# Reordering the loads and casts of the output weights, and the start of the second pair, in a retention and gated-FFN kernel

## The chip, the cores and the metric

The kernel runs on one core of one Trainium2 chip. The metric is the device time of the program in microseconds (us), as the median of several executions. The span that a profile gives, from the first to the last instruction, is about 1.7 us shorter than the time of the same execution (344.3 for 345.99 us in the profile of the kernel before).

Beside each time stands the mean granted clock of TensorE over that execution, as a share of full speed. In this case it turned out to matter: two executions of one kernel on one chip differ by over 7 us, and those that differ have different clocks (346.25 us at 1.0 and 353.74 us at 0.971, both in c_before). I call an execution one at full clock where that mean is 0.999 or 1.0, and compare such executions with each other wherever I explain a difference of the schedule.

## The reference

The first half is retention: attention with a causal mask that decays with distance, without softmax. The second half is a feed-forward net with a sigmoid gate over all 8 × 576 = 4608 tokens.

```python
# q, k, v: (8 batches, 8 heads, 576, 64) float32
scores = scale * q @ k.transpose(0, 1, 3, 2)
gamma = 1.0 - 2.0 ** (-5.0 - np.arange(H))
Dmat = where(rel >= 0, gamma[:, None, None] ** rel, 0.0)   # rel = i - j
attn = (scores * Dmat) @ v
x = attn.transpose(0, 2, 1, 3).reshape(4608, 512)
gate = 1 / (1 + exp(-(x @ w_gate)))          # w_gate, w_val: (512, 1536)
out = (gate * (x @ w_val)) @ w_out           # w_out: (1536, 512)
```

The decay factors into gamma^i on q and gamma^-j on k. So a chunk of 128 tokens needs scaled q and k, a triangular mask, and a running state (the sum of k times v of the chunks before it).

## The kernel before

There are 40 attention steps, one per batch and chunk (the fifth chunk of a batch is only 64 tokens). I count steps and output rows from 0. "Chunk five" is the sixth chunk, that is, step 5. Steps 0 to 3 are done as two pairs at the start, with another layout. Every later step goes through the same supply chain: SyncE loads k, q and v; GpSimd (POOL) scales them to bf16; a transposing DMA turns k and q; then TensorE (PE) multiplies.

All early loads are issued in one fixed order on one queue, through a pool of 18 buffers:

```python
    load_pair(0)
    load_pair(1)
    for f in range(0, NFC, 2):
        load_w(f, 2)            # gate and value weights
    load(4)
    for f in range(6):
        load_wo(f)              # output-weight rows 0 to 5, 256 KB each
    load(5)                     # chunk five
    for f in range(6, NFC):
        load_wo(f)              # output-weight rows 6 to 11
```

The supply chain of a later step, with the turn by DMA:

```python
    def casts_to(s):
        while done["cast"] <= min(NS - 1, s):
            x = done["cast"]
            loads_to(x + (1 if x < 16 else 2))
            cast_k(x)           # POOL, 4 instructions
            cast_q(x)           # POOL
            cross(x)            # DMA transpose of k and q, tile T
            cast_v(x)           # POOL
            done["cast"] += 1
```

Steps 4 and 5 are turned on PE instead (`turn`). The hidden layer of the first 512 tokens runs in two halves of columns, `fill(n)` is n matmuls on zeros that keep PE busy, and the first output stage is this:

```python
    for s in (4, 5):
        cast_k(s); cast_q(s); cast_v(s)
        if s == 4:
            for f in range(6):
                cast_wo(f, on_pool)     # rows 0 to 5 on POOL
    ...
    for fc in range(NFC):
        if fc == 2:
            turn(4, [on_act])
        if fc == 7:
            turn(5, [on_act, on_dve])
        if fc in (4, 6, 8, 9, 10, 11):
            advance(at + 1)             # one phase of steps 4 and 5
        if fc > 5:
            cast_wo(fc, on_act if fc % 2 else on_dve)   # rows 6 to 11, just in time
        for nb in range(4):
            nc.tensor.matmul(opps[nb], lhsT=gvs[fc][:, nb * P:(nb + 1) * P], rhs=wo_sb[:, fc, :],
                             start=(fc == 0), stop=(fc == NFC - 1))
        if fc == 7:
            cast_dense(5, 0)
            cast_dense(5, 1)
```

A phase of kind `st` is a state update: four matmuls on PE, then two copies of the state by VectorE (DVE). So DVE's queue holds, in order, a copy that needs PE, then a cast that PE needs (in the trace of this kernel two copies at 52.70 and 53.15 us, then the cast of an output-weight row at 53.61).

## Time and profile before

| | before |
|---|---|
| time, median of 3 | 349.4 us (348.04 to 349.63) |
| the execution that was profiled | 345.99 us, span 344.3 us, clock 1.0 |
| PE busy | 328.6 us of the span (95%) |
| first output stage on PE | 41.9 to 61.2 us |

There is a tension in the first two rows that the prediction passed over, and it comes back later: the profiled execution is 2 us faster than the fastest of the three timed ones.

Two views carry more than the prediction shows. First lines of the page of the kernel before: the span, the clock that TensorE was granted (tenths of full speed, 40 slices), and the group of the first block's output products (busy time, mean ns of one, then the idle time of the engine just before them and what ended most of it).

```profile
span 344.3 us, 7601 instructions
...
PEclk9999999999999999999999999999999999999999
...
L680 PE MATMUL op<-wo_sb,gv 128*128 128x512 bf16 x48 | 11.9, 378 | 5.8 <-DVE wo_sb L198 2.8
```

The clock was full throughout this execution. PE stood idle for 5.8 us in front of the 48 products of the first output stage, and nowhere else in one group for as long. The list of waits of the first 62 us of the kernel before (total us, times, longest) says for what:

```profile
PE op L680 <- DVE wo_sb L198: 2.8, 2, 1.4
...
PE op L680 <- ACT wo_sb L198: 2.6, 2, 1.4
```

Four waits of 1.2 to 1.4 us, each for the cast of an output-weight row (`wo_sb`), two by DVE and two by ScalarE (ACT).

### The profile page before, as it was taken

What the parts mean: (1) busy time and instruction counts of PE and PEld (TensorE: products, weight loads), DVE (VectorE), ACT (ScalarE), POOL (GpSimd) and SP (SyncE); (2) the same over time, 40 slices, a digit from 0 to 9 for tenths busy, and PEclk for the clock granted to TensorE, in tenths of its full rate; (3) what the DMA queues carried; (4) which work ended last, traced back from release to release, by engine and by line L of the source; (5) the groups of instructions that cost most, each with busy time, mean ns of one, the idle gap of its engine ahead of it and who ended that gap; (6) DMA issues with size and microseconds to landing.
All of it is one profiled execution on the core that took longest, in us unless ns stands there. A gap on an engine that the chain in (4) does not pass through costs nothing.

```text
span 344.3 us, 7601 instructions
## 1 busy us (share of the span) xinstructions
PE 328.6 (95%) x2868; PEld 188.6 (55%) x2868; DVE 167.0 (49%) x350; ACT 171.1 (50%) x352; POOL 186.5 (54%) x333
## 2 busy tenths in 40 slices
PE   7899885998999999999999999999999999999996
PEld 3574342786956656656656655544555455544443
DVE  5758413564747626616527625550575255503320
ACT  6564333665755646436554655454554445324321
POOL 7533759968879885695258985591667500000000
PEclk9999999999999999999999999999999999999999
DMA  8999998999999999999929999992996430020002
GB/s 217 316 347 287 249 270 166 190 170 195 202 197 242 206 219 283 195 236 213 202 79 225 174 209 253 192 186 93 202 194 126 120 82 0 2 91 30 2 30 91
DMA packets 169716, 60.13 MB, mean 175 GB/s; under 512 B 151120, under 2 KB 163664, under 8 KB 169680
## 3 DMA queue, kind: packets, MB, share of 16 engines
q1 hardware_dynamic: 169536, 59.52, 82.6%
q8 instruction: 22, 0.36, 0.5%
q14 instruction: 14, 0.11, 0.2%
q10 hardware_dynamic: 144, 0.13, 0.1%
HBM read 37.75 MB, written 9.44 MB: 137 GB/s over the span
## 4 chain that ended last, share of the span: by engine, by line
PE 89%; ACT 3%; DVE 3%; POOL 2%; issue 1%; DMA 1%; POOLq 0%; ACTq 0%; DVEq 0%
PE h L476 53%; PE op L542 23%; PE op L680 3%; PE pv L400 2%; PE qk L379 2%; PE pv L398 2%; PE st L412 2%; DVE sbd L418 1%; POOL kp L216 1%; DMA k32p<-in_k_dram 1%; PE op L532 1%; PE pvp L362 1%; ACT vs L257 0%; DVE pt L381 0%; ACT sbd L341 0%
## 5 line engine op out<-in xcount | busy, mean ns | idle before, releaser
L476 PE MATMUL h<-xT,wv_sb 128*128 128x512 bf16 (+3 forms) x584 | 117.5, 324 | 0.7 <-ACT g L500 0.7
L476 PE MATMUL h<-xT,wg_sb 128*128 128x512 bf16 (+3 forms) x584 | 117.5, 324 | 0.2 <-DVE gv L504 0.2
L226 POOL TENSOR_TENSOR qk_nat<-k,ktab 64x256 bf16<-64x256 f32 x128 | 78.5, 613 | 54.3 <-PE st L412 27.7
L504 DVE TENSOR_TENSOR gv<-g,h 128x512 bf16<-128x512 bf16 (+1 forms) x106 | 66.3, 626 | 67.6 <-PE h L476 53.7
L500 ACT ACTIVATE g<-h 128x512 bf16<-128x512 f32 (+1 forms) x106 | 58.1, 549 | 75.6 <-PE h L476 68.6
L542 PE MATMUL op<-wo_sb,gv 128*128 128x512 bf16 x360 | 82.8, 379 | 0.0
L418 DVE CAST sbd<-st 64x256 bf16<-64x256 f32 x112 | 47.1, 420 | 50.3 <-PE st L412 47.8
L476 PEld LDWEIGHTS <-wg_sb 128*128 128x128 bf16 x584 | 51.3, 98 | 36.3 <-issue 0.4
L476 PEld LDWEIGHTS <-wv_sb 128*128 128x128 bf16 x584 | 51.1, 98 | 33.7 <-issue 1.0
L247 POOL CAST vbd<-v 64x256 bf16<-64x256 f32 x128 | 50.6, 395 | 14.2 <-PE pv L400 9.3
L542 PEld LDWEIGHTS <-gv 128*128 128x128 bf16 x360 | 33.3, 98 | 35.1
L257 ACT CAST vs<-v 64x256 bf16<-64x256 f32 x112 | 45.1, 403 | 1.7
L514 ACT COPY ob<-op 128x512 f32<-128x512 f32 x33 | 19.2, 585 | 43.4 <-PE op L542 40.8
L236 POOL TENSOR_TENSOR qk_nat<-q,qtab 128x512 bf16<-128x512 f32 (+1 forms) x36 | 37.5, 1043 | 2.8
L402 ACT CAST xT<-pv 128x512 bf16<-128x512 f32 (+1 forms) x36 | 19.3, 537 | 29.0 <-PE pv L400 29.0
L381 DVE TENSOR_TENSOR pt<-qk,tri 128x512 bf16<-128x512 f32 (+1 forms) x36 | 22.6, 629 | 19.9 <-PE qk L379 19.4
L412 PEld LDWEIGHTS <-qk_nat 128*128 128x128 bf16 x224 | 13.9, 98 | 11.4 <-POOL vbd L247 1.3
L400 PE MATMUL pv<-pt,vbd 128*128 128x64 bf16 x256 | 19.1, 193 | 0.6 <-DVE pt L381 0.6
L398 PE MATMUL pv<-T,sbd 128*128 128x64 bf16 x228 | 18.5, 193 | 0.0
L400 PEld LDWEIGHTS <-vbd 128*128 128x128 bf16 x256 | 16.4, 98 | 3.8
L398 PEld LDWEIGHTS <-sbd 128*128 128x128 bf16 x228 | 15.9, 98 | 3.4 <-issue 0.8
L680 PE MATMUL op<-wo_sb,gv 128*128 128x512 bf16 x48 | 11.9, 378 | 5.8 <-DVE wo_sb L198 2.8
(72 smaller groups left out, 176.4 us busy)
## 6 DMA issues: line engine op xcount, KB each, us to landing
out_dram<-ob SPq DMA_DIRECT2D x35, 256.0 KB, 2.4
k<-in_k_dram SPq DMA_DIRECT2D x28, 256.0 KB, 4.1
q<-in_q_dram SPq DMA_DIRECT2D x28, 256.0 KB, 4.7
v<-in_v_dram SPq DMA_DIRECT2D x28, 256.0 KB, 5.1
wg<-in_moe_w_gate_dram SPq DMA_DIRECT2D x12, 256.0 KB, 6.0
wv<-in_moe_w_val_dram SPq DMA_DIRECT2D x12, 256.0 KB, 6.3
wo<-in_moe_w_out_dram SPq DMA_DIRECT2D x12, 256.0 KB, 5.8
k32p<-in_k_dram SPq DMA_DIRECT2D x4, 256.0 KB, 4.4
```

Of the source, the lines that this page charges most:

```text
L226: nc.gpsimd.tensor_tensor(out=kn[half(hh), j, :, half(hh)], in0=k32[half(j), hh::2, :], in1=ktab[half(j), c, hh::2].unsqueeze(2).to_broadc ...
L236: nc.gpsimd.tensor_tensor(out=qs[0:n], in0=q32[0:n], in1=qtab[0:n, c, :].unsqueeze(2).to_broadcast([n, H, D]), op=ALU.mult)
L247: nc.gpsimd.tensor_copy(out=vb[half(hh), j, :, half(hh)], in_=v32[half(j), hh::2, :])
L257: nc.scalar.copy(out=natural["vs", s][half(hh), j], in_=loaded[s][2][half(j), hh::2, :])
L381: nc.vector.tensor_tensor(out=pt[:, :, 0:n].rearrange("p m (j t) -> p m j t", t=64), in0=qkp[:, :, 0:n].rearrange("p m (j t) -> p m j t", ...
L398: nc.tensor.matmul(pvp[:, m, half(j)], lhsT=before[:, m, :], rhs=qT[:, m, half(j)], start=True, stop=False)
L400: nc.tensor.matmul(pvp[:, m, half(j)], lhsT=vb[:, j, m, :], rhs=pt[:, m, half(j)], start=before is None, stop=True)
L418: nc.vector.tensor_copy(out=sb[half(hh), :, half(hh)], in_=st_tiles[b][half(hh)])
L476: nc.tensor.matmul(out, lhsT=w_sb[:, kc, fc * P:(fc + 1) * P], rhs=xT[:, kc, t0 + a:t0 + e], start=(kc == 0), stop=(kc == NKC - 1))
L500: nc.scalar.activation(out=g[:, 0:n], in_=h1[:, 0:n], func=AF.Sigmoid)
L504: nc.vector.tensor_tensor(out=gvs[some[0]][:, a:e], in0=g[:, 0:n], in1=h2[:, 0:n], op=ALU.mult)
L542: nc.tensor.matmul(opp, lhsT=gvs[fc][:, nb * P:(nb + 1) * P], rhs=wo_sb[:, fc, :], start=(fc == 0), stop=(fc == NFC - 1))
```

## The change

The intent: load chunk five ahead of all output weights; take the six casts away from POOL and let DVE and ACT make all twelve, alternating, in the order in which the rows land, and ahead of the copies that wait for PE; do the turns of chunks four and five earlier; and in the second pair, order turns and copies by when their data come, with fewer fill matmuls.

```diff
     load(4)
-    for f in range(6):
-        load_wo(f)
     load(5)
-    for f in range(6, NFC):
+    for f in range(NFC):
         load_wo(f)
@@ second pair @@
-    fill(2)
+    fill(1)
     pair_pv(0, 0, 1)
     pair_pv(0, 1, 0)
-    pair_out(0, 0, on_act)
     cast_pair("q", 1, 0, dve)
     pair_t("k", 1, 1, ffn_psum, "ffn", on_act)
+    pair_t("q", 1, 0, ffn_psum, "ffn", on_act)
     pair_pv(0, 1, 1)
     cast_pair("q", 1, 1, dve)
-    pair_out(0, 1, on_dve)
+    pair_out(0, 0, on_dve)
     pair_st(0, 1)
     tile_sv(1, on_act)
 ...
-    pair_t("q", 1, 0, ffn_psum, "ffn", on_act)
-    fill(3)
     pair_t("q", 1, 1, ffn_psum, "ffn", on_act)
+    pair_out(0, 1, on_act)
     pair_qk(1, 0, qk_psum, "qk")
     pair_qk(1, 1, ffn_psum, "ffn")
-    fill(4)
 ... (a fill(2) later, and one weight cast moved)
@@ hidden layer and first output stage @@
+        if f == 8:
+            for s in (4, 5):
+                cast_k(s); cast_q(s); cast_v(s)
+        if f == 10:
+            cast_wo(0, on_dve)
+            turn(4, [on_act])
 ...
-        if s == 4:
-            for f in range(6):
-                cast_wo(f, on_pool)
 ...
+    cast_wo(1, on_act)
+    cast_wo(2, on_dve)
+    advance(at + 1)
 ...
+    cast_wo(3, on_act)
     for fc in range(NFC):
+        if fc == 1:
+            advance(at + 1)
+            cast_wo(4, on_dve)
         if fc == 2:
-            turn(4, [on_act])
-        if fc == 7:
+            cast_dense(5, 0)
+            cast_dense(5, 1)
+            cast_wo(5, on_act)
+            cast_wo(6, on_dve)
+            cast_wo(7, on_act)
+            cast_wo(8, on_dve)
+        if fc == 4:
             turn(5, [on_act, on_dve])
-        if fc in (4, 6, 8, 9, 10, 11):
+            cast_wo(9, on_act)
+            cast_wo(10, on_dve)
+            cast_wo(11, on_act)
+        if fc in (5, 6, 7, 9):
             advance(at + 1)
-        if fc > 5:
-            cast_wo(fc, on_act if fc % 2 else on_dve)
 ... (the two cast_dense(5, ...) behind row 7 go)
```

More of the change, by code (lines that the diff above doesn't have):

```diff
@@ L625 @@
     pair_pv(1, 0, 0)
+    fill(2)
     pair_pv(1, 0, 1)
     cast_w("v", 0, 2, 0, on_act)
-    cast_w("v", 0, 2, 1, on_dve)
     pair_pv(1, 1, 0)
@@ L631 @@
     pair_pv(1, 1, 1)
+    cast_w("v", 0, 2, 1, on_dve)
     pair_out(1, 1, on_dve)
@@ L652 @@
         next_w(f + 2)
+        if f == 8:
+            for s in (4, 5):
+                cast_k(s)
+                cast_q(s)
+                cast_v(s)
+        if f == 10:
+            cast_wo(0, on_dve)
+            turn(4, [on_act])
         h_first((f + 1,), 0, 4 * P)
@@ L655 @@
             nc.vector.memset(zero.pop(0), 0.0)
-    for s in (4, 5):
-        cast_k(s)
-        cast_q(s)
-        cast_v(s)
-        if s == 4:
-            for f in range(6):
-                cast_wo(f, on_pool)
     done["cast"] = 6
@@ L681 @@
                              start=(fc == 0), stop=(fc == NFC - 1))
-        if fc == 7:
-            cast_dense(5, 0)
-            cast_dense(5, 1)
     for nb in range(4):
```

## The prediction

> **What bounds the kernel now.** I read the page first, then busy time by stretches of 10 us, the list of waits of the first 62 us, the chain that ended last, and the timelines of single engines, with the landing times of the single transfers that the trace keeps beside each issue.
>
> ```profile
> PE 328.6 (95%) x2868; PEld 188.6 (55%) x2868; DVE 167.0 (49%) x350; ACT 171.1 (50%) x352; POOL 186.5 (54%) x333
> ...
> PE   7899885998999999999999999999999999999996
> ```
>
> TensorE is the bound: 328.6 of 344.3 us. Only its idle time, or filler matmuls on its path, can be won, and the digit row (busy tenths of 8.6 us slices) puts the weak spots into the first quarter. By stretches of 10 us (columns: PE, PEld, DVE, ACT, POOL, clock, DMA share, GB/s):
>
> ```profile
> 40.00:50.00 10.00, 9.58 (x70) 5.05 (x69) 2.20 (x4) 2.12 (x5) 7.76 (x14) 1.00 1.06 273
> 50.00:60.00 10.00, 4.88 (x47) 2.57 (x45) 3.66 (x8) 4.45 (x9) 7.64 (x13) 1.00 0.84 162
> 60.00:70.00 10.00, 8.85 (x132) 7.20 (x132) 5.89 (x18) 5.92 (x15) 9.04 (x18) 1.00 1.01 193
> ```
>
> From 50 to 60 us PE does 4.88 us of work. The chain of waits names the cause:
>
> ```profile
> 50.95 0.53 ACT wo_sb L198
> 51.52 1.02 PE op L680 x4
> 52.70 0.42 DVE sbd L418
> 53.15 0.43 DVE sbd L418
> 53.61 0.44 DVE wo_sb L198
> 54.09 1.02 PE op L680 x4
> ```
>
> PE waits for the cast of an output-weight row; that cast stands in DVE's or ACT's order behind a copy that itself waits for PE. There are four such gaps, of 1.39, 1.42, 1.41 and 1.20 us: 5.4 us. The weights were long there: rows 6 to 11 landed at 45.5, 46.2, 46.8, 49.0, 49.7 and 50.4 us, but were cast at 47.1, 50.9, 53.1, 53.6, 57.3 and 59.6. It is an order problem, not a transfer problem.
>
> The second place is the start of the hidden layer:
>
> ```profile
> 16.04 1.04 PE L132 MATMUL idle<-blank 128*128 128x512 bf16 x4
> ...
> 18.71 0.43 DVE L193 CAST wv_sb<-wv 128x512 bf16<-128x512 f32 x1 [0.69 <-DMA wv<-in_moe_w_val_dram]
> ...
> 20.26 0.61 PE L476 MATMUL h<-xT,wg_sb 128*128 128x256 bf16 x4
> ```
>
> Filler matmuls stand before the second pair's last state update, and the first weights end landing at 18.69 us, 1.57 us before PE uses them.
>
> [...] a 256 KB tile of k, q or v (256-byte packets) lands every 1.0 to 1.2 us, an output-weight tile (2 KB packets) every 0.66 to 0.76. [...] SyncE issues the transpose of step 11 (count from 0) at 84.15 us, just after POOL's scaling of that step's q ends at 84.12. [...]
>
> **The change, part by part.**
>
> (a) *Second pair.* Fillers go from 2+3+4 to 1+2 in this stretch, six fewer, but most fill waits. The four before the state update (16.04 to 17.08) are on the path and go; the turn of the second q comes about 1 us earlier, so I place the state update near 15.6 instead of 17.0 and its pair's last products near 18.2. The first hidden group then waits for landed weights: DVE cast done near 19.1. So the hidden layer starts effectively at 18.7 instead of 20.26: 1.5 us. The single gap at 36.88 (0.69 us) may go or stay.
>
> (b) *Load order.* Chunk five (the sixth) moves ahead of all output weights. Its three tiles took 3.24 us to land (41.56 to 44.80). The fifth chunk's v lands at 37.63, so the sixth is there near 40.9 and output row 0 near 41.5 (before: 38.10), then one row per 0.67 us: row 5 near 45, row 11 near 49 to 50.5, since the bytes before it are the same. The first output product, at 41.88 before, needs row 0: 41.5 + 0.43 for the cast. What (a) won is therefore lost in a wait for row 0; the output stage starts at 42, as before.
>
> (c) *Casts.* Six POOL casts of 0.61 us (3.4 us together) leave POOL, six more go to DVE and ACT. POOL had 3.39 us of waiting for k at 51.65, so this frees nothing on the path. All casts now stand ahead of the copies that wait for PE. The stage then takes PE's own time: 48 matmuls in groups of four at 0.865 us (10.4), the turn of chunk five (0.65), and its scores, states and values (about 0.9), plus some 1 us of waiting for the fourth step's masked scores and the first rows: 13 us, so PE ends it at 55 to 56 instead of 61.32. Shift there: 5.3 to 6.3 us.
>
> (d) *What that shift meets.* Every later attention step needs a chain: load, POOL casts, transpose by DMA. It starts with the load of step 6, behind the last output row in both kernels; k landed at 51.52, and I expect 50.5 to 51.5. From there POOL works without a break to step 9:
>
> ```profile
> 51.65 2.85 POOL L226 TENSOR_TENSOR qk_nat<-k,ktab 64x256 bf16<-64x256 f32 x4 [3.39 <-DMA k<-in_k_dram]
> ...
> 63.06 2.63 POOL L226 TENSOR_TENSOR qk_nat<-k,ktab 64x256 bf16<-64x256 f32 x4
> ...
> 80.36 2.64 POOL L226 TENSOR_TENSOR qk_nat<-k,ktab 64x256 bf16<-64x256 f32 x4 [0.40 <-DMA k<-in_k_dram]
> ```
>
> Then it waits for k of step 10, landed at 74.36 behind the eighth step's transpose, and of step 11 (80.20). None of this depends on how fast PE is. So the chain gains at most what k of step 6 gains, about 0.5 us. The slack before PE's use, landing of the turned tile to first score matmul: step 7: 65.64 to 72.11, 6.5 us; step 8: 70.56 to 76.03, 5.5; step 9: 77.32 to 83.22, 5.9; step 10: 83.60 to 87.63, 4.0; step 11: 90.45 to 93.69, 3.2; step 12: 94.82 to 102.62, 7.8; later ones over 8.
>
> ```profile
> 84.15 2.74 SPq L263 DMA_TRANSPOSE T<-qk_nat  x1
> ...
> 93.69 0.40 PE L379 MATMUL qk<-T 128*128 128x64 bf16 x8
> ```
>
> The least slack decides: step 11 lets PE come 3.2 us earlier plus the chain's own 0.5. Of 5.3 to 6.3 us won, 1.6 to 2.6 come back as waits for turned tiles between 70 and 92 us. After that PE runs at its own rate to the end. The sum is −3.7 us: 349.4 − 3.7 = 345.7 us, 1.1% less.
>
> **The rivals.** *The chain follows and the whole shift stays:* then 343.1 to 344.1, and with the 0.69 us gap gone too somewhat less. For it: POOL loses 3.4 us of casts and the loads are issued from fewer freed buffers late. Against it: POOL was waiting for data just then, and the transfer share was 1.06 from 40 to 50 us, so no earlier landing is in sight. *The output weights become the bound:* if row 0 lands at 43 or a late row blocks DVE ahead of the state copies (row 10 at 49.7 in the old trace), the stage ends at 57; step 11 still decides, so this costs little unless it delays the load of step 6; with step 6 a microsecond late the result is 346.7. *Nothing gained:* moving the weights behind chunk five could starve the first products by all of its 3.24 us and the in-order queues of ACT and DVE, now full of casts waiting for landings, could hold up sigmoids; then 348 to 350. Against it: each row lands in 0.67 us, products need 0.865 us per row.
>
> **Range and chances.** Centre 345.7. The low end takes most of the shift and an earlier step 6 (343.4), the high end a later one and a stall of 1 us that I missed (347.8). Faster by over 2% needs under 342.4 us, 7.0 us, more than the whole of the shift at the output stage: 0.07. Slower by 2% needs a new wait of 10 us: 0.01.
>
> **What would show it.** In the profile after: the hidden layer starts 1 to 2 us earlier; PE waits for output row 0 near 40 to 42 us; no wait of PE for output-weight casts over 0.5 us once the stage runs; busy PE in 50 to 60 us over 8.5 us; POOL still starts step 6 at 50.5 to 51.7; new PE waits, ended by the transposes, of together 1.6 to 2.6 us before the scores of steps 8 to 11. I am wrong if k of step 6 lands over 1.5 us earlier or later, if turned tiles land earlier by the whole shift, or if PE has a gap of over 2 us before the first output product.

## The result, and the profile after

| | before | after |
|---|---|---|
| median | 349.12 us (348.04 to 349.63, 4 runs) | 339.69 us (338.85 to 340.25, 4 runs) |
| ratio of fast runs | | 0.9732 (0.97 to 0.9763) |
| profiled execution, span | 344.3 us, clock 1.0 | 338.5 us, clock 1.0 |
| PE begins the hidden layer | 20.26 us | 19.35 us |
| first output product | 41.88 us | 41.76 us |
| PE begins the next hidden layer | 61.16 us | 55.39 us |

A ratio is the mean time of one kernel's fast runs over that of the other's of the same rounds, so it is not quite the ratio of the medians. A run counts as slow, and is left out of the ratio, when it is over 1.5% above the fastest of its kernel.

The change is faster by 2.7%; I had given that 7 chances in 100. The time is 3.7 us below the low end of the range (343.4).

Page of the kernel after, the lines that answer to those of before:

```profile
span 338.5 us, 7556 instructions
...
PE   7899989889999999999999999999999999999996
...
PEclk9999999999999999999999999999999999999999
```

The slice with busy digit 5 (51.6 to 60.2 us) is gone. Busy time by stretches of 10 us of the kernel after, with the same columns as in the prediction:

```profile
40.00:50.00 10.00, 8.88 (x70) 4.67 (x69) 4.83 (x11) 6.98 (x13) 4.81 (x8) 1.00 1.03 336
50.00:60.00 10.00, 9.87 (x121) 7.16 (x121) 5.08 (x15) 4.20 (x10) 7.76 (x14) 1.00 1.01 193
60.00:70.00 10.00, 9.06 (x156) 7.29 (x155) 6.45 (x19) 7.30 (x18) 9.12 (x17) 1.00 0.91 174
```

From 50 to 60 us PE now works 9.87 us, where it worked 4.88. The list of waits of its first 62 us:

```profile
DVE wo_sb L196 <- DMA wo<-in_moe_w_out_dram: 5.2, 6, 1.4
...
ACT wo_sb L196 <- DMA wo<-in_moe_w_out_dram: 3.1, 3, 2.0
...
PE pv L398 <- DVE pt L379: 0.9, 1, 0.9
```

The casts now wait for the landing of their row, and no line has PE waiting for a cast of an output-weight row any more. Within the stage PE keeps one wait of 0.9 us, for the masked scores of step 4. Single instructions of the kernel after, in its timeline (start, duration, engine, line, operation, and in brackets the idle time before it and what ended that):

```profile
17.93 0.43 DVE L191 CAST wv_sb<-wv 128x512 bf16<-128x512 f32 x1 [0.52 <-DMA wv<-in_moe_w_val_dram]
...
19.35 0.61 PE L474 MATMUL h<-xT,wg_sb 128*128 128x256 bf16 x4
...
41.28 0.43 DVE L196 CAST wo_sb<-wo 128x512 bf16<-128x512 f32 x1 [1.09 <-DMA wo<-in_moe_w_out_dram]
...
41.76 1.25 PE L691 MATMUL op<-wo_sb,gv 128*128 128x512 bf16 x4
...
43.97 0.19 PE L398 MATMUL pv<-pt,vbd 128*128 128x64 bf16 x1 [0.92 <-DVE pt L379]
...
70.26 0.40 PE L377 MATMUL qk<-T 128*128 128x64 bf16 x8
...
87.91 0.40 PE L377 MATMUL qk<-T 128*128 128x64 bf16 x8
```

So far this is nearly the profile that I had predicted. One line is missing: PE was to wait for output row 0, and the list has no such wait. The scores of step 4 begin at 41.41 us, the first product stands at 41.76, and the cast of row 0 ends at 41.28 + 0.43 = 41.71, so row 0 can have cost PE about 0.2 us. The last two lines are the surprise: they are the first score matmuls of steps 8 and 11, at which I expected PE to stand still, and no wait is in front of either. The whole 5.77 us that PE won by the end of the stage (61.16 to 55.39) are still there at the end: 344.3 − 338.5 = 5.8. The trace's records of single transfers show why there was no wait:

| | before: landed, used, slack | after: landed, used, slack |
|---|---|---|
| turned tile of step 8 | 70.56, 76.03, 5.5 us | 70.02, 70.26, 0.2 us |
| turned tile of step 9 | 77.32, 83.22, 5.9 | 75.92, 77.44, 1.5 |
| turned tile of step 10 | 83.60, 87.63, 4.0 | 80.94, 81.86, 0.9 |
| turned tile of step 11 | 90.45, 93.69, 3.2 | 87.49, 87.91, 0.4 |
| k of step 10 (loaded) | 74.36 | 71.66 |

Step 8's tile comes 0.5 us earlier, as I had said of all of them. Those of steps 9, 10 and 11 come 1.4, 2.7 and 3.0 us earlier. PE just gets by, with 0.2 us to spare at step 8 and 0.4 at step 11.

The step at which the chain came forward most is the tenth. POOL's first scaling of its k, before and after, in the two timelines:

```profile
74.52 2.63 POOL L226 TENSOR_TENSOR qk_nat<-k,ktab 64x256 bf16<-64x256 f32 x4 [2.78 <-PE pv L400]
...
71.82 2.64 POOL L224 TENSOR_TENSOR qk_nat<-k,ktab 64x256 bf16<-64x256 f32 x4 [0.63 <-DMA k<-in_k_dram]
```

The view ends the first wait by PE, which would be another cause: POOL held up by PE itself. The trace's records speak against it. POOL's semaphore instruction that waits for this k ends at 74.43 us, 0.07 us behind its landing, and the scaling starts 0.10 us later, just as at 51.65 and 80.36 us, where the view names k. So both waits ended with the landing of k.

Two questions remained. Why did the chain of loads and turns come earlier, when POOL began it only 0.2 us earlier (51.46 for 51.65)? And why do the times differ by 349.12 − 339.69 = 9.4 us, but the profiles by 5.8 us?

### The profile page after: what moved, and what is told of

The parts are those of the page before. It is cut to its first block, busy times and chain, and to the rows that moved or that the text cites. A ratio compares the mean times of both kernels' runs of the same rounds, so it can differ in the third digit from the quotient of the medians.

```text
span 338.5 us, 7556 instructions
## 1 busy us (share of the span) xinstructions
PE 325.6 (96%) x2829; PEld 187.8 (55%) x2862; DVE 168.5 (50%) x353; ACT 172.5 (51%) x355; POOL 183.2 (54%) x327
## 4 chain that ended last, share of the span: by engine, by line
PE 83%; DMA 7%; issue 2%; ACT 2%; POOL 2%; DVE 1%; SPq 1%; POOLq 0%; ACTq 0%
PE h L474 49%; PE op L540 23%; DMA q<-in_q_dram 2%; PE pv L398 2%; PE pv L396 2%; DMA wo<-in_moe_w_out_dram 2%; PE qk L377 2%; PE st L410 2%; DMA k32p<-in_k_dram 2%; PE op L691 1%; POOL qk_nat L224 1%; DMA k<-in_k_dram 1%; SPq L91 1%; PE op L530 1%; ACT vs L255 1%
## 5 line engine op out<-in xcount | busy, mean ns | idle before, releaser
L540 PE MATMUL op<-wo_sb,gv 128*128 128x512 bf16 x345 | 81.6, 379 | 0.8
L512 ACT COPY ob<-op 128x512 f32<-128x512 f32 x33 | 19.2, 585 | 44.3 <-PE op L540 38.6
L410 PE MATMUL st<-vs,qk_nat 128*128 128x64 bf16 x224 | 15.6, 193 | 1.5 <-DVE sbd L416 0.8
```

Of the source, the lines that this page charges most:

```text
L410: nc.tensor.matmul(st_tiles[b][:, m, :], lhsT=natural["k", s][:, j, m, :], rhs=natural["vs", s][:, j, m, :], start=(c == 0 and j == 0 and ...
L540: nc.tensor.matmul(opp, lhsT=gvs[fc][:, nb * P:(nb + 1) * P], rhs=wo_sb[:, fc, :], start=(fc == 0), stop=(fc == NFC - 1))
```

## The experiments

Twelve kernels ran, four at a time on one chip (chips 10, 14 and 11), each four beside runs of the kernel before on the same chip. By the ratio of fast runs and the bound of 2%, each of these kernels comes out as the same as the kernel before or as unclear (e_fetch_before, a single run, has no ratio), and kernels of different sets ran on different chips. So the times carry only the larger differences below, and the smaller ones rest on the traces. Where I give a median at full clock, it is that of the runs with a mean clock of 0.999 or more.

### The kernel before once more (c_before)

No edit; this asks how much the times of one kernel spread, and in what.

> The kernel before, unchanged, as a control. Its profiled execution on record took 346.0 us, its timed runs 348.0 to 349.6; the changed kernel's profile and timed runs agree (340.3 and 338.9 to 339.7). Theory A (a matter of the chip or of the occasion): here profile and timed runs agree with each other within 1 us, wherever they lie. Theory B (the kernel before has executions of two lengths, whose difference arises in the chain of loads, casts and transposes between 50 and 95 us): here some run lies near 346 and some near 349, or the profile shows longer waits of PE between 60 and 95 us than the one on record, 1.65 us in gaps over 0.2 us.

It ran 20 times: median 349.67 us, from 346.25 to 353.74, ratio 1.0004 (0.9965 to 1.0043). The spread lies in the clock. Of all 89 runs of the kernel before in the three sets, 19 were at full clock, 28 near 0.995, 42 lower. In the largest set (39 runs) the medians of the three groups were 346.28, 348.42 and 351.09 us. The profile of this run fell into a low one, with a span of 349.7 us. Its clock row, from its page:

```profile
PEclk9999995699999999999999999999999999999999
```

And by stretches of 5 us, of the same run (the three last columns are clock, share of DMA, GB/s):

```profile
50.00:55.00 5.00, 1.84 (x19) 1.11 (x17) 2.04 (x4) 3.66 (x7) 2.84 (x5) 0.87 0.90 190
55.00:60.00 5.00, 4.07 (x20) 1.76 (x19) 1.54 (x4) 0.00 (x0) 4.57 (x9) 0.50 0.92 165
60.00:65.00 5.00, 3.34 (x19) 1.57 (x19) 0.42 (x1) 1.31 (x3) 4.55 (x9) 0.50 1.20 216
```

In the middle of the output stage, where PE works only 1.84 of 5 us, the clock drops to 0.50. The records have it at half from 53.7 to 67.4 us, 13.65 us. From 50.31 us to the drop at 53.72 PE worked 1.39 us, and its longest gap until then was 1.39 us. What sets off a drop, and why only in some executions, is not shown: in the profile on record PE worked 2.18 us from 50 to 55 us, little more than here, and the clock stayed at 1.00. The means of whole runs fit stretches at half clock: 13.65 us of them take 0.5 × 13.65 / 349.7 = 0.02 off the mean of this run, which is 0.98. Turned round, a mean of 0.995 over 346 us would be about 0.005 × 346 / 0.5 = 3.5 us at half clock, an estimate from the means of the runs. That is the middle group, and it costs about 2.1 us by the group medians (348.42 − 346.28).

So a prediction that shifts the median 349.4 by what a profile at full clock shows mixes two states. The base of that profile is about 346.1 us.

### The second pair alone (e_pair_only)

The kernel before, with only the second pair's new order (the middle part of the diff above).

```diff
-    fill(2)
+    fill(1)
 ...
+    pair_t("q", 1, 0, ffn_psum, "ffn", on_act)
 ...
-    fill(3)
 ...
-    fill(4)
```

> The kernel before with only the second pair's new order and fills. The hidden layer began 0.91 us earlier in the changed kernel. If starts early are handed on through the four order gaps of the output stage, this run is 0.7 to 1.2 us faster than before; if they are lost in a wait (rows of output weights, chunk five), 0 to 0.3 us faster. My prediction (lost only because of the new load order) says here: about 0.9 faster.

Median 347.87 us over 20 runs (344.74 to 352.74), ratio 0.9931 (0.9896 to 0.9966). At full clock it is 345.2 us against 346.28 of before: 1.1 us won. Eleven of the 20 runs were in the lowest clock group (16 of 39 of the kernel before beside it), so there is no sign that the pair's order helps the clock. The clock row of its page:

```profile
PEclk9759999999999999999999999999999999999999
```

Here the clock dropped near the start (half from 12.3 to 26.0 us, again 13.65 us), in the second pair, where PE is also patchy (busy tenths of 7 and 7 in the first two slices of 8.7 us on that page). So in this kernel at least, the four gaps of the output stage are not the only place that can set it off.

### Everything but the second pair (e_casts_only)

The kernel after, with the second pair as it was before.

```diff
-    fill(1)
+    fill(2)
 ...
-    pair_t("q", 1, 0, ffn_psum, "ffn", on_act)
 ...
+    fill(3)
 ...
+    fill(4)
```

> The changed kernel with the second pair put back as it was. If row 0 of the output weights (landed at 41.3 us) sets the start of the output stage, the early start is lost anyway and this run equals the changed kernel within 0.3 us; if not, it is 0.7 to 1.2 us slower than the changed one. Against the kernel before it should be 8 to 9.4 us faster.

Median 341.31 us (340.59 to 342.84, 4 runs, two at full clock), ratio 0.9807 (0.9719 to 0.9896). At full clock, 340.6: 5.7 us under before. So the loads and casts are the bulk, and the pair adds 1.1 us by e_pair_only, or 0.8 by what this kernel lacks to the changed one (339.85 at full clock, on another chip). By the profiles it is 0.4: spans of 338.9 and 338.5. The expectation asked for 0.3 or less, or 0.7 or more, so it is not decided.

### The change with the old order of loads (e_old_loads)

```diff
     load(4)
+    for f in range(6):
+        load_wo(f)
     load(5)
-    for f in range(NFC):
+    for f in range(6, NFC):
         load_wo(f)
```

> The changed kernel with the old order of loads: chunk five behind six rows of output weights. Row 0 then lands near 38 us instead of 41.3, but chunk five near 44.8 instead of 40.6. Theory: the output stage starts 1 to 1.5 us earlier, waits for chunk five's turn (its q is cast by about 46.5), and ends within 0.7 us of the changed kernel's 55.4 us; total within 1 us of it. Rival (the load order is what the change is about): 2 us or more slower than the changed kernel.

Median 340.76 us (340.02 to 341.05, all four at full clock), ratio 0.9774 (0.9706 to 0.9843). The order of the loads is a small part of the gain: under 1 us against the changed kernel, which ran on another chip, so I put no exact figure on it. What is lost is in its list of waits from 40 to 95 us:

```profile
PE qk L379 <- DMA T<-qk_nat: 1.0, 2, 0.6
```

Two waits for turned tiles, of 0.39 us before the scores of step 8 and 0.58 before those of step 11: the very places that I had predicted, and of about half the size.

### The changed kernel once more (c_after)

> The changed kernel, unchanged, as a control beside the others of this call. Expected 339 to 340.3 us, mean clock 0.995 or more in nearly every run, about 6.5 us below those runs of the kernel before whose clock is 1.0.

Median 340.02 us: 339.83, 339.85 and 340.19 at full clock, and one of 344.04 at 0.98. Ratio 0.9802 (0.9717 to 0.9887); it is nearer to 1 than on record because of that one run, and because the filter took the slowest runs of before out. The changed kernel can fall into the low clock too, in one of the eight runs that I have of it, where the kernel before is at full clock in 19 of 89.

### The gaps filled with worthless work (e_warm)

The kernel before, with matmuls on zeros put just into the four gaps of the output stage: 6, 6, 6 and 5 of them, into banks that are free there. If the low clock comes from the gaps, the kernel gets faster although it does more.

```diff
+    def fill(n, psum=ffn_psum, tag="ffn"):
 ...
+        if fc in (7, 8, 10):
+            fill(6, pv_psum, "pv")
+        if fc == 11:
+            fill(5, qk_psum, "qk")
         for nb in range(4):
             nc.tensor.matmul(opps[nb], ...
```

> The kernel before with filler matmuls (6, 6, 6 and 5) put into the four gaps of the output stage, where PE waits anyway; nothing else changed. Throttle theory (the gaps make the TensorE clock drop to half [...], after the gaps, in many executions): the share of runs with a clock of 0.995 or less falls to about half or lower, and the median falls from about 348.6 to 346.3 to 347.3 us, while the fastest runs stay at 346.1. Rival (the drops are an affair of the chip, not of the gaps): the same spread as before, median within 0.5 us of it. Rival (drops come from the first 20 us): the same too.

Median 346.81 us (345.89 to 348.8, 20 runs), while the kernel before in the same set had 349.48 (23 runs); ratio 0.9945 (0.9919 to 0.9972), with fast runs alone and so without the slowest of before. No run of the 20 is in the lowest group, and 16 are at full clock or 0.999; of before, 4 of 23 were at full clock and 12 in the lowest group. At full clock it is 0.6 us slower than before (346.71 for 346.12); 23 fill matmuls that don't quite fit the gaps would do that, which no run separates. The stretches of 5 us of this kernel:

```profile
50.00:55.00 5.00, 4.51 (x32) 2.23 (x30) 1.90 (x4) 3.65 (x7) 4.60 (x8) 1.00 0.92 175
55.00:60.00 5.00, 4.84 (x44) 2.54 (x43) 2.01 (x4) 0.10 (x1) 4.56 (x8) 1.00 0.96 197
```

PE is busy, with nothing useful, and the median falls by 2.7 us. That is the second term of the gain, and it is shown: the four gaps cost 5.4 us themselves, and some 3 us more in the median by the clock.

### Only the late casts moved (e_rows_early)

The kernel before, with the casts of rows 6 to 11 put ahead: three before the products of row 4, three behind the turn of chunk five. Loads, POOL's casts and the pair stay.

```diff
+        if fc == 4:
+            cast_wo(6, on_dve)
+            cast_wo(7, on_act)
+            cast_wo(8, on_dve)
         if fc == 7:
             turn(5, [on_act, on_dve])
+            cast_wo(9, on_act)
+            cast_wo(10, on_dve)
+            cast_wo(11, on_act)
 ...
-        if fc > 5:
-            cast_wo(fc, on_act if fc % 2 else on_dve)
```

> The kernel before with only the casts of output rows 6 to 11 moved ahead of the copies that wait for PE; loads, second pair and POOL's casts as before. If the order of these six casts is the whole matter: the four gaps go, the output stage ends near 56 us instead of 61.3, the fastest runs are near 341 (346.1 less 4.5 to 5.5), and clock drops become rare: median 341 to 342, so 7 us or more under the kernel before. If the load order or POOL's relief is needed, less than half of that.

Median 342.69 us (three of four at full clock, these 342.23; one 344.83 at 0.99), ratio 0.9872 (0.9797 to 0.9946). At full clock that is 3.9 us won of the 5.4 us of gaps, with six casts moved; I had expected 4.5 to 5.5. The rest is a new gap, in its timeline:

```profile
52.99 0.28 PE L412 MATMUL st<-vs,qk_nat 128*128 128x64 bf16 x4 [1.77 <-ACT vs L257]
```

ACT now has its casts in front of the copies of v for step 5's state. The changed kernel moves those copies to before row 2, and this gap isn't there.

### The masked scores ahead of a cast (e_mask_first)

The changed kernel still waits 0.92 us at 43.04 for DVE, which masks step 4's scores behind the cast of row 2. Exchange the two:

```diff
     cast_wo(1, on_act)
-    cast_wo(2, on_dve)
     advance(at + 1)
+    cast_wo(2, on_dve)
```

> The changed kernel with the fourth step's scores and mask put ahead of the cast of output row 2 on DVE: the wait of 0.92 us before that step's values (at 43 us) goes. If tiles turned by DMA for steps 8 and 11 now decide (0.24 and 0.4 us of slack in the changed kernel's trace), 0 to 0.4 us faster than the changed kernel and new waits before scores; if the supply follows PE, 0.9 us faster.

The wait is gone and the stage ends 0.86 us earlier (54.49 for 55.35 in c_after, the changed kernel on the same chip). The span is 338.0 for 338.5. The median is 339.66 us (339.46 to 340.1, all at full clock), ratio 0.9766 (0.9719 to 0.9812), against 339.85 of c_after at full clock. Of the 0.86 us, 0.5 arrives in the span and 0.2 in the median. Step 8's scores start at 69.36, 0.25 us after their tile landed (69.11), and before those of step 11 PE waits 0.21 us. This beats the kernel before, and all others here by a hair; over the changed kernel, 0.2 us is not resolved.

### Moving the instruction fetches, after (e_fetch)

The trace of the kernel before had, besides the kernel's own transfers, blocks of 16 KB on another queue, which its page lists as `q8 instruction: 22, 0.36, 0.5%`. There are 22 of them after the change too. That they bring PE's instructions is my reading of the traces. PE runs 2868 matmuls and 2868 weight loads in the kernel before, which would be 5736 / 22 = 261 to a block (an estimate from these two counts). And the blocks keep step with PE: the sixth, seventh and eighth start when PE has begun 1518, 1752 and 1984 of its recorded instructions in the kernel before (at 77.66, 88.20 and 98.66 us), and 1500, 1733 and 1962 in the changed one (at 71.67, 82.51 and 92.73 us). I call them fetches. In the kernel before one came at 72.1 to 73.3 us, when k of step 10 was under way, and one at 88.2, when step 11's turn was. That k took 6.03 us from issue to landing; k of step 12, issued at 81.71 with no fetch in its way, took 3.54.

To move the fetches and little else, the start of the changed kernel gets 50 tiny matmuls for 3 fill matmuls. That is 94 more PE instructions (47 matmuls, each with its weight load), so by this reading every later fetch should fall earlier against the work.

```diff
-    fill(12)
+    fill(9)
+    tiny = ffn_psum.tile([P, 512], FP32, tag="ffn", name="tiny")
+    for i in range(50):
+        nc.tensor.matmul(tiny[0:64, 0:64], lhsT=blank[0:64, 0:64], rhs=blank[0:64, 0:64], start=True, stop=True)
```

> The changed kernel with 50 tiny matmuls in place of 3 of the 12 opening fillers: 94 more PE instructions ahead of everything, so PE's blocks of instructions (16 KB each, fetched by the transfer engines) are fetched about 2.6 us earlier everywhere: near 69 us instead of 71.8, near 79 instead of 82. Theory (the tile in flight when such a block is fetched lands 1.5 to 2 us late): the turned tile of step 8 lands near 71 instead of 69.3 us, PE waits 0.5 to 1.2 us for it, step 10's k is on time or late by the same; total 0.5 to 1.5 us slower at full clock. Rival (landing times are noise of the occasion): landings as in the changed kernel within 0.5 us, total within 0.3.

The fetches came at 61.4, 70.8 and 79.8 us (64.8, 71.8 and 82.1 in c_after). Span 340.3 us, median 342.09 (two runs at full clock, 341.0 and 342.03; two at 0.98 to 0.99), ratio 0.9807 (0.9737 to 0.9878). k of step 10 now took 5.90 us to land (67.98 to 73.88), where c_after had 3.99 (67.11 to 71.10). Step 8's tile landed at 71.50 (69.31), step 10's at 83.61 (80.30). PE's score matmuls in the timeline of this kernel:

```profile
71.54 0.41 PE L380 MATMUL qk<-T 128*128 128x64 bf16 x8 [0.59 <-DMA T<-qk_nat]
...
83.66 0.41 PE L380 MATMUL qk<-T 128*128 128x64 bf16 x8 [1.11 <-DMA T<-qk_nat]
```

There they are, 1.70 us of waits for turned tiles, in the order of the 1.6 to 2.6 that I had predicted, in a kernel that differs from the changed one mainly by where its instruction blocks fall. It isn't quite a clean exchange: the edit also delays the start (the stage ends at 55.92 for 55.35). Of the 1.86 us in span, 0.57 are that, and 1.29 arise after the stage.

### Moving the instruction fetches, before (e_fetch_before)

The same edit in the kernel before, one look.

> The same 50 tiny matmuls in the kernel before. On record its blocks were fetched at 72.1, 77.7 and 88.2 us, and k of step 10 landed at 74.36, the turned tile of step 11 at 90.45. Theory: with fetches 2 to 3 us earlier, k of step 10 lands within 4.5 us of its issue (6.0 on record), and the slack before step 11's scores is 5 us or more instead of 3.2. Rival (the late landing belongs to the transfers themselves): 6 us again, slack 3 to 3.5. [...]

346.35 us at full clock in the one run, which is nothing: this kernel has slack. But the landings moved without any change to the loads, the casts or the schedule. The fetches came at 65.6, 75.6 and 83.7 us. k of step 10 took 3.76 us (6.03 on record) and landed at 72.93 (74.36). Step 11's turned tile landed at 88.42 (90.45), and its slack grew from 3.2 to 5.6 us. In the profile of c_before, where the low clock had put the fetch at 77.1 us, k of step 10 took 4.04 us and landed at 72.41. So the landing times that I had taken for the supply chain's own were the chain's plus a fetch that PE's own progress places.

All 14 traces of this case say the same of k of step 10. It took over 5 us to land in the three in which a fetch began more than 1 us before it landed (6.03 before, 5.90 in e_fetch, 5.08 in e_warm), and 3.76 to 4.12 in the eleven others.

### Fewer products in the stage (e_short)

Is there a limit of supply at all? The changed kernel with 10 of the 48 output products of the stage left out. The result is wrong on purpose (relative error 0.17).

```diff
-        for nb in range(4):
+        for nb in range(2 if fc in (6, 7, 8, 9, 10) else 4):
```

> The changed kernel with 10 of the 48 first output products left out (a wrong result on purpose): PE ends the output stage 2.16 us earlier, everything else alike. Theory of my prediction (the turned tiles of steps 8 to 11 set a limit; in the changed kernel 0.24 to 0.9 us of slack are left): the total falls by 0.2 to 1.0 us, and 1.2 to 2 us of new waits appear before scores of steps 8 to 11. Rival (the supply follows PE): the total falls by 2.0 to 2.2 us.

PE ends the stage at 53.68 us, 1.67 us before c_after (55.35), and the time hardly moves: span 338.1 us (338.5 in c_after, on another chip), median 340.12 (339.83 to 341.31, two of four at full clock; ratio 0.9752, 0.9687 to 0.9816). Pieces of the chain of waits of this kernel (start, length, what):

```profile
67.66 4.00 DMA k<-in_k_dram
...
76.11 5.02 DMA T<-qk_nat
81.17 0.41 PE qk L377 x8
...
81.72 5.74 DMA T<-qk_nat
87.51 0.41 PE qk L377 x8
```

k of step 10, the turn of that step, its scores, the next turn, its scores: PE now waits 1.22 us before the scores of step 8, 0.59 before step 10's and 0.11 before step 11's, 1.9 us in all. This is the term of my prediction, at the size at which I had put it (1.6 to 2.6), but it begins only where the changed kernel ends. Of a further gain in the output stage at most about half a microsecond arrives (0.3 us of 1.67 here, 0.5 of 0.86 in e_mask_first) until the chain of loads and turns is earlier.

### Everything combined (e_best)

The changed kernel with the masked scores first, two output rows ahead of chunk five, the load of step 6 ahead of rows 8 to 11 with these rows cast late, and the first pair's state copy one place later. It was to bring the chain forward together with PE.

```diff
     load(4)
+    load_wo(0)
+    load_wo(1)
     load(5)
-    for f in range(NFC):
+    for f in range(2, 8):
+        load_wo(f)
+    load(6)
+    for f in range(8, NFC):
         load_wo(f)
 ...
+        if fc in (6, 7):
+            cast_wo(2 * fc - 4, on_dve)
+            cast_wo(2 * fc - 3, on_act)
```

> A try at more: mask first (as in the run of that name); rows 0 and 1 of the output weights ahead of chunk five; step 6's load ahead of rows 8 to 11, whose casts come after step 5's scores; the second pair's second q copied ahead of the state copy. If supply and row 0 are both relieved, step 6's k lands near 48.5 instead of 51.3 us and the total falls 0.7 to 1.5 us below the changed kernel; if rows 8 to 11 then come late for PE, it is equal or slower by up to 1 us.

A miss. Median 341.21 us (341.06 to 341.84, clocks 0.998 to 1.0), ratio 0.9783 (0.9707 to 0.9858), about 1.2 us slower than the changed kernel on another chip (340.02). Its list of waits from 40 to 62 us has the cause:

```profile
PE op L695 <- DVE wo_sb L201: 1.4, 1, 1.4
```

The late rows now come too late for the products, at 51.02 us. This is the gap of the kernel before in another guise: the last rows decide the stage, and three tiles of k, q and v stand in front of them in the queue, as chunk five's did, which took 3.24 us to land.

## Why the prediction was wrong

By its own steps:

- **(a) Second pair: mechanism right in part, size smaller.** The state update came at 15.89 us (I had put it at 15.6). But its last products ended near 19.2 and not 18.2, since from the update to the hidden layer it is 3.46 us, as it was 3.26 before: I had squeezed that stretch without a reason in the trace. The hidden layer begins at 19.35, so 0.9 us earlier and not 1.5. It did not wait for weights, as I had expected: DVE's cast was done at 17.93 + 0.43 = 18.36. By itself the pair is worth 1.1 us. The gap of 0.69 us stayed (0.68 at 35.96).
- **(b) Load order: landings right, the wait wrong.** v of chunk five landed at 40.59 us (predicted 40.9), row 0 at 41.25 (41.5), row 11 at 50.10 (49 to 50.5). The stage began at 41.76 (42), but not for the reason that I gave, "What (a) won is therefore lost in a wait for row 0". PE waited about 0.2 us for row 0. The pair's 0.9 us went into the turn of chunk four (39.23 to 39.68 us) and the scores of step 4 (41.41), which the change puts ahead of the first product. I had left both out, so the hit at 42 is partly luck.
- **(c) Casts: right.** (Two of the old cast times stand in the wrong order: row 8 was cast at 53.6 us and row 9 at 53.1.) The wait for masked scores was 0.92 us ("some 1 us"), the stage ended at 55.39 (55 to 56), the shift is 5.77 us (5.3 to 6.3).
- **(d) What the shift meets: wrong.** The step was "None of this depends on how fast PE is. So the chain gains at most what k of step 6 gains, about 0.5 us." POOL's part of it held: it started step 6 at 51.46 us. But k of step 10 and what follows it gained 2.7 to 3.0 us. In the one trace that I had, that k was under way while a block of PE's instructions was fetched. When PE runs ahead, its fetches run ahead too: those at 72.1 and 77.7 us are at 64.8 and 71.7 after the change. The second fell on v of step 10 (5.6 us from issue to landing), which nobody waits for so early, and k of step 10 took 3.84 us instead of 6.03: with an issue 0.5 us earlier, that is the 2.7 us. (The turn of step 11 meets a fetch in both kernels, at 88.2 and 82.5.) e_fetch and e_fetch_before show this in both kernels. e_short shows that the rule of the least slack itself was sound. The waits of 1.6 to 2.6 us therefore measured 0. That they are quite gone is partly luck, with 0.2 and 0.4 us to spare: e_fetch has such waits before the scores of steps 8 and 10, and e_old_loads before those of 8 and 11. (One reading of the list of slacks is wrong, without effect: "later ones over 8" does not hold for steps 16, 17, 25 and 26, which have 7.0, 7.6, 7.4 and 6.9 us.)
- **The base: wrong.** "349.4 − 3.7 = 345.7" took a shift from a profile at full clock off a median of runs that mostly weren't. The sum lacked a term: the gaps don't only cost their length, they also lower the clock (4 of 23 runs at full clock with them, 16 of 20 with them filled). Before, that is 349.1 − 346.1 = 3.0 us in the median; the changed kernel has none of it at the median. c_before and e_warm show it.

The sum, set right: 346.1 at full clock, less 5.8 that arrive whole, is 340.3, as the profiled run of the changed kernel has it (340.25; the median of its four is 0.6 lower). From 349.1 that is 3.0 + 5.8 + 0.6 = 9.4 us. Of the miss of 6.0 us (345.7 to 339.7), 3.3 is the base (349.4 for 346.1), about 2.1 the waits that did not come (5.8 for 3.7), and 0.6 the spread of single runs.

Of the rivals, *the chain follows and the whole shift stays* came true in its second half: the whole shift stayed. The chain followed only in part, by 0.5 us at step 8 and 3.0 at step 11 of a shift of 5.77, and the slack took up the rest. I had argued against it that POOL was waiting for data just then and that the transfers were full from 40 to 50 us (a share of 1.06). Both are true and both concern the load of step 6, which came only 0.2 us earlier; the chain moved 20 us later, at step 10. The reasons that I gave for this rival, POOL's 3.4 us and the freed buffers, are not what the traces show.

What is only argued: I have not shown by which means a fetch of 16 KB holds up a tile of 256 KB by about 2 us. No run here separates it. That the dip at the start of e_pair_only comes from the gaps there is likely, but not tested.

## What to carry to other kernels

Before adding a shift to a time, ask whether the profile and the time are of the same state: here the profiled run was 2 us faster than every timed one, and this said that a term was missing. A row of short gaps can cost more than its length, once directly and once by the clock (here 5.4 us of gaps, and some 3 us more in the median); worthless work in the gaps is a cheap test for that (here it took 2.7 us off the median). And a slack that is read from one trace holds only with that trace's coincidences: ask what was in flight at that moment and whether it moves with the engine that you are about to speed up.
